# Chunked attention and a gated feed-forward layer: transposes of tiles 14 to 23 by transfers on SP's queue, memory rows on GpSimd's queue, last product in 384 + 128 columns

## Chip, core and metric

The kernel runs on one core of a Trainium2 chip. The metric is the device time of one execution in microseconds; the median of several runs is given. A core has TensorE (matmul; PE in the profile, with its weight loads apart as PEld), VectorE (DVE), ScalarE (ACT), GpSimd (POOL) and SyncE (SP). SP and GpSimd issue transfers, which 16 DMA engines carry out.

## What is computed

Attention in chunks of 32 queries, each over 8 memory keys and a window of 16 + 32 + 8 keys, and then a feed-forward layer over all tokens:

```python
# B, H, S, D = 4, 8, 768, 64; chunk 32, left 16, right 8, n_mem 8
for c in range(S // 32):
    q_c = q[:, :, c_start:c_end]
    k_full = concatenate([mem_k, k[:, :, l_start:r_end]], axis=2)
    v_full = concatenate([mem_v, v[:, :, l_start:r_end]], axis=2)
    scores = scale * matmul(q_c, k_full.T)
    a = exp(scores - max(scores)); a = a / (sum(a) + 1e-09)
    out[:, :, c_start:c_end] = matmul(a, v_full)
x = out.transpose(0, 2, 1, 3).reshape(3072, 512)
result = (maximum(x @ w_gate, 0) * (x @ w_val)) @ w_out      # w_gate, w_val 512x1536, w_out 1536x512
```

## The kernel before

The 3072 tokens are 24 tiles of 128, six to a batch. **Attention of a tile a** has these steps, each one operation of the planner (lines 400 to 428):

- q and k of the tile are loaded by GpSimd's queue, cast to bf16 (`load_qk`, line 185; 18 buffers).
- `t`: four transposes on TensorE into PSUM (`qk_t`, line 206, matmul line 210), one set for k (i = 1) and one for q (i = 0).
- `tc`: a copy from PSUM by ACT or DVE into qT, or into kT with gaps for the memory keys (`qk_copy`, line 212; the copies show as lines 75 and 77).
- `s`: scores (line 236), 32 small products; they need q and k of the tile and k of the next one in the batch.
- maximum, difference, exponential, sum, reciprocal and normalisation on DVE and ACT (lines 241 to 279).
- `p` and `pc`: four transposes of the normalised probabilities (line 285) and the copy from PSUM (`p_copy`, line 287; six buffers).
- `v` and `x`: values (line 298), 16 products against a block-diagonal v, and the copy into xT (`x_copy`, line 301; two buffers, one for each block in work).

The block-diagonal v (`v_bd`, two sets, by batch in turn) is filled by loads on GpSimd's queue (line 167), and its eight memory rows by copies within SBUF on SP's queue, eight for a batch (`mem_rows`, line 138; batch 0 gets its rows from a pattern).

**The feed-forward part** works on blocks of tiles, `BLOCKS = [3, 3, 4, 4, 4, 4, 2]`. For each of twelve hidden columns m of a block there are four products for the gate and four for the value (`first`, line 317, matmul line 323), a relu on ACT (line 329) and a gating product on DVE (line 335). After them come, for each tile of the block, twelve products with w_out (`second`, line 339, matmul line 344, 512 columns wide), a copy on ACT and a store on SP's queue (`store`, line 347; three buffers). The columns of blocks 0 and 1 are worked in turn, in groups of three, as the weights arrive. Four PSUM buffers hold these products, two (`aps`) the transposes, memory keys and values, and one the scores.

**The order** is made by a planner in Python (`schedule`, line 524) while the program is built: each operation has an engine, a cost, what it depends on, a priority and the buffers that it takes and gives. The planner keeps a clock, and an engine that is free takes the ready operation of the best priority; attention (1) comes before feed-forward products (2). On TensorE an attention operation has to have been ready for `MARGIN = 0.4` us after 36 us. The order that results is fixed on each engine: on the chip an engine works its own list and waits where something is late. GpSimd's loads follow a list of their own (lines 481 to 519), with a booked time in the queue for each: 1.05 us for a tile of q or k. `pace` (line 396) holds the transposes of a tile back, in the planner's clock alone, until a column of the block before is at hand:

```python
def pace(a):
    blk = block_of[a]
    return [("f", blk - 1, NDC * (a - starts[blk]) // BLOCKS[blk], 0)] if blk > 1 else []
```

SP's list holds the loads at the start, the memory rows of batches 1 to 3 and the 24 stores.

Of the kernel before, what the change touches and what calls it, by code (L numbers as in the profile page):

```python
# [20 lines left out]
def kernel(  # L21
# [31 lines left out]
    EARLY = TPB  # L53
# [5 lines left out]
    ldpool = ctx.enter_context(tc.tile_pool(name="ldpool", bufs=18))  # L59
    kvpool = ctx.enter_context(tc.tile_pool(name="kvpool", bufs=2))  # L60
# [77 lines left out]
    def mem_rows(b):  # L138
        for par in range(2):
            p = slice(64 * par + CTX, 64 * par + CTX + NMEM)  # L140
            for hp in range(HP):
                src = vmem[p, b, HP * par + hp]
                nc.sync.dma_start(
                    v_bd[b % NSET][p, hp, :, D * par:D * par + D],
                    bass.AP(tensor=src.tensor, offset=src.offset,
                            ap=[src.ap[0], [0, NCH], [1, D]]))
# [59 lines left out]
    def qk_t(a, i):  # L206
        ps = TMP["qk", a, i] = aps.tile([128, HP, 128], BF16, tag="aps", name="qk_ps")
        x = qk_b.pop((a, i))
        for hp in range(HP):
            nc.tensor.transpose(ps[:, hp, :], x[:, 2 * hp:2 * hp + 2, :].rearrange("p h d -> p (h d)"), ident_b)  # L210

# [74 lines left out]

    def p_copy(a, eng):
        PT[a] = smpool.tile([128, HP, 128], F16, name="pT", bufs=6)
        copy(eng, PT[a], TMP.pop(("p", a)))
# [49 lines left out]
    def second(blk, t, m0):  # L339
        st = FFN[blk]  # L340
        if m0 == 0:
            st["o", t] = fps.tile([128, DM], F32, tag="fps", name="out_ps")
        for m in range(m0, m0 + MS):
            nc.tensor.matmul(st["o", t], lhsT=st["gv"][:, m, 128 * t:128 * t + 128],  # L344
                             rhs=w_out_sb[:, m, :], start=(m == 0), stop=(m == NDC - 1))

    def store(blk, t, eng):
        o = opool.tile([128, DM], F32, name="o_sb")
        copy(eng, o, FFN[blk].pop(("o", t)))
        row = 128 * (starts[blk] + t)  # L350
        nc.sync.dma_start(out[row:row + 128, :], o)
# [9 lines left out]
            "qk": 18, "xT": 2, "gv": 2, "gr": 3, "o": 3, "kv": 2}  # L361
# [29 lines left out]
    for b in range(B):  # L391
        op(("new", b), {"DVE": 0.4}, lambda e, b=b: new_batch(b), ["kmc"], take=["kv"],
           prio=(-4.5,) if b == 0 else (1, TPB * b - 2, 0), after=[("t", TPB * b - 2, 0)] if b else [])


    def pace(a):
        blk = block_of[a]
        return [("f", blk - 1, NDC * (a - starts[blk]) // BLOCKS[blk], 0)] if blk > 1 else []

    for a in range(NT):  # L400
        b, t = divmod(a, TPB)
        last = t == TPB - 1
        for i in (1, 0):
            op(("t", a, i), {"PE": 0.24}, lambda e, a=a, i=i: qk_t(a, i), [("qk", a, i), "ib", ("new", b)],
               (1, a - i, 0), ["aps"], ["qk"], pace(max(a - i, 0)))
            op(("tc", a, i), psum(HP * 128), lambda e, a=a, i=i: qk_copy(a, i, engine[e]), [("t", a, i)],
               (1, a - i, 0), (), ["aps"])
        op(("s", a), {"PE": 0.36}, lambda e, a=a: scores(a),
           [("tc", a, 0), ("tc", a, 1)] + ([] if last else [("tc", a + 1, 1)]), (1, a, 1), ["sps"],
           ["kv"] if last else [], [("s", a - 1)] if a else [])  # L410
        op(("max", a), {"DVE": 0.74 + (0.2 if t == 0 or last else 0)}, lambda e, a=a: row_max(a), [("s", a)],
           (1, a, 2), ["mx"])
        op(("sub", a), {"DVE": 0.74}, lambda e, a=a: subtract(a), [("max", a)],
           (1, a, 3), ["dif"], ["sps", "mx"])
        op(("exp", a), {"ACT": 1.15}, lambda e, a=a: exponent(a), [("sub", a)], (1, a, 4), ["p"], ["dif"])
        op(("sum", a), {"DVE": 0.74}, lambda e, a=a: row_sum(a), [("exp", a)], (1, a, 5), ["sm"])
        op(("rec", a), {"DVE": 0.24}, lambda e, a=a: reciprocal(a), [("sum", a)], (1, a, 6), ["rinv"], ["sm"])
        op(("nrm", a), {"DVE": 0.74}, lambda e, a=a: normalise(a), [("rec", a)], (1, a, 7), ["pn"], ["p", "rinv"])
        op(("p", a), {"PE": 0.24}, lambda e, a=a: p_t(a), [("nrm", a)], (1, a, 8), ["aps"], ["pn"])
        op(("pc", a), psum(HP * 128), lambda e, a=a: p_copy(a, engine[e]), [("p", a)], (1, a, 9), ["pT"], ["aps"])  # L420
        blk = block_of[a]
        j = a - starts[blk]
        op(("v", a), {"PE": 0.45}, lambda e, a=a: values(a),
           [("pc", a)] + [("vl", b, 0 if b else t // 3, n) for n in range(2 if b else 2 * HP)]
           + ([("mr", b)] if b else []), (1, a, 10), ["aps"] + (["xT"] if j == 0 else []), ["pT"],
           [("v", a - 1)] if a else [])
        op(("x", a), psum(HP * 128), lambda e, a=a: x_copy(a, engine[e]), [("v", a)], (1, a, 11), (), ["aps"],
           [("x", a - 1)] if a else [])


    seq = [(blk, m) for g in range(WG) for blk in range(2) for m in range(GM * g, GM * g + GM)]
    seq += [(0, None), (1, None)]
    for blk in range(2, len(BLOCKS)):
        seq += [(blk, m) for m in range(NDC)] + [(blk, None)]
    for rank, (blk, m) in enumerate(seq):
# [11 lines left out]
        else:  # L447
            for t in range(n):
                for m0 in range(0, NDC, MS):
                    op(("o", blk, t, m0), {"PE": MS * 0.216}, lambda e, blk=blk, t=t, m0=m0: second(blk, t, m0),  # L450
                       [("g", blk, m) for m in range(m0, m0 + MS)] + [("wo", 0 if m0 + MS <= NDC // 2 else 1)], (2, rank, t, m0),
                       ["fps"] if m0 == 0 else [], ["gv"] if (t, m0) == (n - 1, NDC - MS) else [],
                       [("o", blk, t, m0 - MS)] if m0 else [("o", blk, t - 1, NDC - MS)] if t else [])
                op(("oc", blk, t), {"ACT": psum(512)["ACT"]}, lambda e, blk=blk, t=t: store(blk, t, engine[e]),
                   [("o", blk, t, NDC - MS)], (0.5, rank), ["o"], ["fps", ("o", 2.5)])


    def load_qk_op(a, i):
        load(("qk", a, i), 1024, 1.05, lambda: load_qk(a, i), take=["qk"])

    def load_v_op(b, half, par, c0, c1, n, deps, after):
        for i, part in enumerate(reversed(v_parts(b, par, c0, c1))):
            rows = part[3] - part[2]
            load(("vl", b, half, n) if i == 0 else ("vx", b, n), rows * (part[5] - part[4]),
                 rows * (part[5] - part[4]) * 1.15e-3, lambda part=part: load_v_rows(*part), deps, (), after)
# [7 lines left out]
    def load_w_op(g):  # L473
        for w in range(2):
            for par in range(2):
                load(("w", g, w, par), 256, 1.03, lambda g=g, w=w, par=par: load_gate_val(g, w, par))
# [4 lines left out]
    late = [(a, i) for a in range(TPB, NT) for i in (1, 0)]  # L481
    for a, i in ((0, 1), (1, 1), (0, 0)):
        load_qk_op(a, i)
    load("ident", 0, 0, lambda: make_identity(nc, ident_h))
    for a, i in ((1, 0), (2, 1), (2, 0), (3, 1)):
        load_qk_op(a, i)
    load_v_half(0, (0, 1))
    for a, i in ((3, 0), (4, 1)):
        load_qk_op(a, i)
    load_v_half(0, (2, 3))  # L490
    for a, i in ((4, 0), (5, 1), (5, 0)):
        load_qk_op(a, i)
    load_w_op(0)
    load_v_half(1, range(HP))
    load_w_op(1)
    load_zero(0)
    load_w_op(2)
    load_zero(1)
    for a, i in late[:3]:
        load_qk_op(a, i)  # L500
    load_zero(2)
    load_w_op(3)
    load_zero(3)
    for par in range(2):
        load(("vm", par), 256, 0.3, lambda par=par: mem_values(par))
    for a, i in late[3:6]:
        load_qk_op(a, i)
    for i in range(2):
        load(("wo", i), 768, 4.1, lambda i=i: load_out(i))
    for a, i in late[6:9]:  # L510
        load_qk_op(a, i)
    for b in range(1, B):
        deps = [("z", HP - 1)] if b < NSET else [("v", TPB * (b - NSET + 1) - 1)]
        op(("mr", b), {"SP": 5.8}, lambda e, b=b: mem_rows(b),
           deps + [(("vm", 0), 0.2)] + ([("s", TPB * b - 3)] if b >= NSET else []), (0,))
        for par in range(2):
            load_v_op(b, 0, par, 0, HP * NCH, par, [], deps)
        for a, i in late[9 + 12 * (b - 1):21 + 12 * (b - 1)]:
            load_qk_op(a, i)

    def timed(d):
        return isinstance(d, tuple) and len(d) == 2 and isinstance(d[1], float)

    def schedule():
# [29 lines left out]
        while len(started) < len(ops) + len(loads):  # L554
            t = heapq.heappop(times)
            while times and times[0] <= t + 1e-9:
# [6 lines left out]
            while moved:  # L563
                moved = False
                for e in ("POOL", "PE", "ACT", "DVE", "SP"):
# [18 lines left out]
                    else:  # L584
# [17 lines left out]
                        done[key] = end + (0.25 if e == "PE" else 0.08)  # L602
                        fn = lambda o=o, e=e: o["fn"](e)
# [51 lines left out]
```

## Time and profile before

| | |
|---|---|
| median of 3 runs | 254.91 us (254.59 to 255.48) |
| profiled execution: span from first to last instruction | 253.9 us |
| profiled execution: its own time around the span | not on the page |
| mean granted TensorE clock | 0.990 |
| TensorE busy | 233.7 us (92%) |
| DVE, ACT, POOL busy | 140.6, 112.6, 90.0 us |
| chain of work that ended last | PE 71%, POOL 16%, DMA 9% |
| transfers issued by GpSimd (q0) | 106400 packets, 16.61 MB |
| transfers issued by SP (q1) | 8624 packets, 6.97 MB |

The page divides the span into 40 slices of 6.35 us and gives each engine's busy share in tenths. The chain of work follows the last instruction back to what released it. A group of instructions has its count, busy time, mean length, and the idle time of its engine ahead of it with what ended it. SP's and GpSimd's instructions that issue transfers are listed as they are worked; the packets of the transfers stand apart, by queue.

### The profile page before, as it was taken

To read this page: it belongs to the slowest core of one execution; us is meant where nothing else is said; L and a number is where in the kernel's file an instruction comes from. 1 tells how busy PE (TensorE), PEld (TensorE's weight loads), DVE (VectorE), ACT (ScalarE), POOL (GpSimd) and SP (SyncE) were. 2 spreads that over 40 slices of the span, in tenths; PEclk is the share of its full clock that TensorE was granted. 3 is DMA by queue.
4 is the path that set the end of the run, shared out by engine and by line. 5 is a ranking of instruction groups with operands and counts; after the bars stand their busy time and mean duration, and the time that the engine had idled before them with its cause. 6 is when DMAs were issued, how large, how long until landed. Compare 5 with 4: busy or idle time off the path is not lost.

```text
span 253.9 us, 6022 instructions
## 1 busy us (share of the span) xinstructions
PE 233.7 (92%) x2517; PEld 131.2 (52%) x2517; DVE 140.6 (55%) x259; ACT 112.6 (44%) x245; POOL 90.0 (35%) x102
## 2 busy tenths in 40 slices
PE   1777759999899899999999999999999999999993
PEld 0666435666554544554544555545455545454871
DVE  3977662578563238786157886168873174810430
ACT  3465543455334334554253553355345345432421
POOL 8999699994125565588010000000000000000000
PEclk9999998999999999999999999999999999999998
DMA  9999999999999999999992001210001200002102
GB/s 71 103 117 138 159 144 174 156 147 187 144 143 186 183 174 140 138 147 121 157 216 29 0 3 41 85 41 3 0 3 64 104 0 3 1 26 102 43 3 83
DMA packets 115052, 23.97 MB, mean 94 GB/s; under 512 B 106320, under 2 KB 111952, under 8 KB 115024
## 3 DMA queue, kind: packets, MB, share of 16 engines
q0 software_dynamic: 106400, 16.61, 93.8%
q1 hardware_dynamic: 8624, 6.97, 9.6%
q8 instruction: 20, 0.33, 0.6%
q14 instruction: 8, 0.07, 0.1%
HBM read 33.24 MB, written 6.29 MB: 156 GB/s over the span
## 4 chain that ended last, share of the span: by engine, by line
PE 71%; POOL 16%; DMA 9%; issue 1%; DVE 1%; ACT 0%; POOLq 0%
PE out_ps L344 24%; PE v_ps L323 19%; PE g_ps L323 19%; POOL qk_b L189 6%; DMA qk_b<-in_k_dram 6%; DMA v_bd<-in_v_dram 3%; PE xT_ps L298 3%; PE qk_ps L210 3%; POOL v_bd L167 3%; POOL v_bd L115 2%; POOL w_gate_sb L101 2%; POOL w_val_sb L101 2%; PE s_ps L236 2%; PE pT_ps L285 1%; DVE xT L77 1%
## 5 line engine op out<-in xcount | busy, mean ns | idle before, releaser
L323 PE MATMUL g_ps<-xT,w_gate_sb 128*128 128x512 f16 (+2 forms) x336 | 76.7, 351 | 1.3 <-DMA w_gate_sb<-in_moe_w_gate_dram 1.3
L323 PE MATMUL v_ps<-xT,w_val_sb 128*128 128x512 f16 (+2 forms) x336 | 76.6, 351 | 0.9 <-DMA w_val_sb<-in_moe_w_val_dram 0.8
L335 DVE TENSOR_TENSOR gvT<-v_ps,g_relu 128x512 f16<-128x512 f32 (+2 forms) x84 | 51.6, 614 | 43.9 <-PE v_ps L323 30.5
L329 ACT ACTIVATE g_relu<-g_ps 128x512 f16<-128x512 f32 (+2 forms) x84 | 45.0, 536 | 62.7 <-PE g_ps L323 52.5
L344 PE MATMUL out_ps<-w_out_sb,gvT 128*128 128x512 f16 x288 | 66.1, 379 | 0.0
L323 PEld LDWEIGHTS <-w_gate_sb 128*128 128x128 f16 x336 | 31.9, 98 | 28.8 <-issue 2.1
L323 PEld LDWEIGHTS <-w_val_sb 128*128 128x128 f16 x336 | 31.1, 98 | 23.6 <-DMA w_val_sb<-in_moe_w_val_dram 1.0
L344 PEld LDWEIGHTS <-gvT 128*128 128x128 f16 x288 | 26.9, 98 | 28.9
L167 POOL DMA_DIRECT2D v_bd<-in_v_dram x24 | 27.8, 1179 | 6.1 <-issue 5.4
L189 POOL DMA_DIRECT2D qk_b<-in_k_dram x24 | 23.0, 957 | 18.4 <-issue 6.8
L189 POOL DMA_DIRECT2D qk_b<-in_q_dram x24 | 22.5, 938 | 13.9 <-PE qk_ps L210 7.9
L75 ACT COPY o_sb<-out_ps 128x512 f32<-128x512 f32 x24 | 14.0, 584 | 28.9 <-PE out_ps L344 28.7
L264 ACT ACTIVATE p_exp<-dif 128x256 f16<-128x256 f32 (+2 forms) x72 | 19.6, 338 | 11.4 <-DVE dif L256 11.3
L210 PE MATMUL qk_ps<-ident_b,qk_b 128*128 128x128 bf16 x192 | 18.3, 227 | 5.0 <-DMA qk_b<-in_k_dram 2.6
L249 DVE TENSOR_REDUCE mx<-s_ps 128x8 f32<-128x512 f32 x24 | 16.5, 688 | 5.9 <-PE s_ps L236 5.6
L77 DVE CAST xT<-xT_ps 128x512 f16<-128x512 f32 x10 | 6.9, 692 | 21.7 <-PE xT_ps L298 21.6
L210 PEld LDWEIGHTS <-qk_b 128*128 128x128 bf16 x192 | 13.3, 101 | 10.8 <-DMA qk_b<-in_k_dram 3.7
L268 DVE TENSOR_REDUCE sm<-p_exp 128x8 f32<-128x512 f16 x24 | 16.3, 680 | 3.4 <-ACT p_exp L264 3.4
L75 ACT COPY pT<-pT_ps 128x512 f16<-128x512 f16 x19 | 11.1, 585 | 12.8 <-PE pT_ps L285 12.8
L279 DVE TENSOR_TENSOR p_n<-p_exp,rinv 128x512 f16<-128x512 f16 x24 | 16.5, 687 | 0.4
L256 DVE TENSOR_TENSOR dif<-s_ps,mx 128x512 f32<-128x512 f32 x24 | 16.4, 684 | 0.3
L298 PEld LDWEIGHTS <-v_bd 128*128 128x128 f16 x384 | 12.8, 96 | 5.5 <-issue 2.3
(39 smaller groups left out, 131.8 us busy)
## 6 DMA issues: line engine op xcount, KB each, us to landing
out_dram<-o_sb SPq DMA_DIRECT2D x24, 256.0 KB
v_bd<-in_v_dram POOLq DMA_DIRECT2D x5, 672.0 KB, 14.0
qk_b<-in_k_dram POOLq DMA_DIRECT2D x24, 128.0 KB, 7.0
qk_b<-in_q_dram POOLq DMA_DIRECT2D x24, 128.0 KB, 7.5
w_gate_sb<-in_moe_w_gate_dram POOLq DMA_DIRECT2D x8, 192.0 KB, 4.7
w_val_sb<-in_moe_w_val_dram POOLq DMA_DIRECT2D x8, 192.0 KB, 6.2
w_out_sb<-in_moe_w_out_dram POOLq DMA_DIRECT2D x2, 768.0 KB, 10.0
v_bd<-in_v_dram POOLq DMA_DIRECT2D x15, 84.0 KB, 5.1
```

What stands on the lines that cost most here:

```text
L75: nc.scalar.copy(o, i)
L167: nc.gpsimd.dma_start(dst[64 * par + s0:64 * par + s1, c0:c1, D * par:D * par + D], bass.AP(tensor=v.tensor, offset=v[b, HP * par, 0, 0].o ...
L189: nc.gpsimd.dma_start(qk_b[a, i], bass.AP(tensor=x.tensor, offset=x[b, 0, 128 * t, 0].offset, ap=[[D, 128], [S * D, H], [1, D]]))
L210: nc.tensor.transpose(ps[:, hp, :], x[:, 2 * hp:2 * hp + 2, :].rearrange("p h d -> p (h d)"), ident_b)
L249: nc.vector.reduce_max(SM[a, "mx"], s4, axis=AX.X)
L264: nc.scalar.activation(p[:, :, :, s0:s0 + k1 - k0], dif[:, :, :, k0:k1], ACT.Exp, scale=SCALE)
L279: nc.vector.tensor_tensor(out=P_n[a], in0=SM.pop((a, "p")), in1=rinv_b, op=ALU.mult)
L298: nc.tensor.matmul(ps[:, hp, r], lhsT=v_bd[b % NSET][:, hp, 4 * t + g, :], rhs=x[:, hp, r], start=True, stop=True)
L323: nc.tensor.matmul(ps, lhsT=w[:, f, 128 * m:128 * m + 128], rhs=xTs[blk][:, f, :], start=(f == 0), stop=(f == NFC - 1))
L329: nc.scalar.activation(st["r", m], st.pop((0, m)), ACT.Relu)
L335: nc.vector.tensor_tensor(out=st["gv"][:, m, :], in0=st.pop((1, m)), in1=st.pop(("r", m)), op=ALU.mult)
L344: nc.tensor.matmul(st["o", t], lhsT=st["gv"][:, m, 128 * t:128 * t + 128], rhs=w_out_sb[:, m, :], start=(m == 0), stop=(m == NDC - 1))
```

## The change

- Tiles 14 to 23: the `t` and `p` steps become transposing transfers from SBUF to SBUF, issued by SP (`qk_dma`, `p_dma`), and no longer TensorE transposes. q goes into qT directly and p into its buffer, without a copy. k goes into a new buffer (`k_t`, three of them), from which ACT or DVE copies it into kT. The planner books 1.3 us of SP for each, and counts the data as there 2.0 us (`LANDING`) after that.
- Memory rows of batches 2 and 3 are issued by GpSimd, ahead of the v loads of their batch, in place of SP; those of batch 1 stay on SP, as eight operations and not one.
- `pace` lets the transposes of a tile begin eight columns earlier (`LEAD`), counted through the blocks; from block 2 on, as before.
- The last tile's products with w_out are made in 384 columns and then in 128, each with its own copy and store. The store is an operation of its own on SP for all tiles.
- The planner's booked times for loads are smaller (0.87 us for q or k, 0.94 in place of 1.15 ns for each row piece of v, 0.99 in place of 1.03 us for weights), and SP's transfers are added to the queue's booked time. The loads' list is written as a text; apart from the memory rows its order is the same.

```diff
-    EARLY = TPB
+    LEAD = [8, 8, 8, 8, 8, 8, 8, 8]
+    LAST = ((0, 384), (384, 512))
+    BY_DMA = 14
+    BY_DMA_P = 14
+    LANDING = 2.0
...
+    ktpool = ctx.enter_context(tc.tile_pool(name="ktpool", bufs=3))
...
-    def mem_rows(b):
-        for par in range(2):
+    def mem_rows(b, eng, pieces):
+        for par, hp in pieces:
             p = slice(64 * par + CTX, 64 * par + CTX + NMEM)
...
+            src = vmem[p, b, HP * par + hp]
+            eng.dma_start(
...
+    def qk_dma(a, i):
+        b, t = divmod(a, TPB)
+        x = qk_b.pop((a, i)).rearrange("p h d -> p (h d)")
+        if i == 0:
+            o = qT[b][:, :, 128 * t:128 * t + 128]
+        else:
+            o = TMP["qk", a, i] = ktpool.tile([128, HP, 128], BF16, name="k_t")
+        nc.sync.dma_start_transpose(o, x)
...
+    def p_dma(a):
+        PT[a] = smpool.tile([128, HP, 128], F16, name="pT", bufs=6)
+        nc.sync.dma_start_transpose(PT[a], P_n.pop(a).rearrange("p h a s -> p (h a s)"))
...
-    def second(blk, t, m0):
+    def second(blk, t, m0, cols):
...
-            nc.tensor.matmul(st["o", t], lhsT=st["gv"][:, m, 128 * t:128 * t + 128],
-                             rhs=w_out_sb[:, m, :], start=(m == 0), stop=(m == NDC - 1))
...
+            nc.tensor.matmul(st["o", t, cols], lhsT=st["gv"][:, m, 128 * t:128 * t + 128],
+                             rhs=w_out_sb[:, m, slice(*cols)], start=(m == 0), stop=(m == NDC - 1))
...
-        return [("f", blk - 1, NDC * (a - starts[blk]) // BLOCKS[blk], 0)] if blk > 1 else []
+        if starts[blk] < TPB:
+            return []
+        m = NDC * (blk - 1) + NDC * (a - starts[blk]) // BLOCKS[blk] - LEAD[blk]
+        return [("f", *divmod(max(m, 0), NDC), 0)]
...
+            if a < BY_DMA:
...
+            else:
+                op(("t", a, i), {"SP": 1.3}, lambda e, a=a, i=i: qk_dma(a, i), [("qk", a, i), ("new", b)],
+                   (1, a - i, 0), ["kt"] * i, [("qk", LANDING)])
+                if i:
+                    op(("tc", a, i), {"ACT": 0.62, "DVE": 0.3}, lambda e, a=a, i=i: qk_copy(a, i, engine[e]),
+                       [(("t", a, i), LANDING)], (1, a - i, 0), (), ["kt"])
+                else:
+                    op(("tc", a, i), {"PE": 0.01}, lambda e: None, [(("t", a, i), LANDING)], (1, a - i, 0))
...
+            op(("p", a), {"SP": 1.3}, lambda e, a=a: p_dma(a), [("nrm", a)], (1, a, 8), ["pT"], [("pn", LANDING)])
+            op(("pc", a), {"PE": 0.01}, lambda e: None, [(("p", a), LANDING)], (1, a, 9))
...
+            if blk == len(BLOCKS) - 1:
+                pieces[-1:] = [(n - 1, cols) for cols in LAST]
...
+                if b == 1:
+                    op(("mr", b, par, hp), {"SP": 0.72}, lambda e, b=b, x=(par, hp): mem_rows(b, nc.sync, [x]),
+                       batch_deps(b) + [(("vm", 0), 0.2), (("vm", 1), 0.2)], (0, par, hp))
+                else:
+                    load(("mr", b, par, hp), 192, 0.2, lambda b=b, x=(par, hp): mem_rows(b, nc.gpsimd, [x]),
+                         batch_deps(b) + [("vm", 0), ("vm", 1)])
...
+    MOVE = {"t": 1.25, "p": 1.25, "mr": 0.2, "os": 0.7}
...
+                        if e == "SP" and key[0] in MOVE:
+                            queue_end = max(queue_end, t) + MOVE[key[0]]
```

More of the change, by code (lines that the diff above doesn't have):

```diff
@@ L52 @@
     BLOCKS = [3, 3, 4, 4, 4, 4, 2]
-    EARLY = TPB
+    LEAD = [8, 8, 8, 8, 8, 8, 8, 8]
[3 more added lines that the diff above has]
+    LANDING = 2.0
+    LOADS = """k0 k1 q0 i q1 k2 q2 k3 v00 v01 q3 k4 v02 v03 q4 k5 q5 w0 v10 v11 v12 v13 w1 z0 w2 z1
+               k6 q6 k7 z2 w3 z3 m q7 k8 q8 o0 o1 k9 q9 k10 b1 q10 k11 q11 k12 q12 k13 q13 k14
+               q14 k15 q15 k16 m2 b2 q16 k17 q17 k18 q18 k19 q19 k20 q20 k21 q21 k22 m3 b3 q22 k23 q23"""
     KEY_RUNS = ((0, CH, 0), (KW, 64, CH), (CH, KW, CTX))
@@ L136, in mem_values @@
         )
-    def mem_rows(b):
-        for par in range(2):
+    def mem_rows(b, eng, pieces):
+        for par, hp in pieces:
             p = slice(64 * par + CTX, 64 * par + CTX + NMEM)
[L141 to L146, printed above, removed]
+            src = vmem[p, b, HP * par + hp]
+            eng.dma_start(
+                v_bd[b % NSET][p, hp, :, D * par:D * par + D],
+                bass.AP(tensor=src.tensor, offset=src.offset,
+                        ap=[src.ap[0], [0, NCH], [1, D]]))
     def pattern_load():
@@ L337, with out_copy, store @@
     MS = 3
-    def second(blk, t, m0):
+    def second(blk, t, m0, cols):
         st = FFN[blk]
         if m0 == 0:
-            st["o", t] = fps.tile([128, DM], F32, tag="fps", name="out_ps")
+            st["o", t, cols] = fps.tile([128, cols[1] - cols[0]], F32, tag="fps", name="out_ps")
         for m in range(m0, m0 + MS):
-            nc.tensor.matmul(st["o", t], lhsT=st["gv"][:, m, 128 * t:128 * t + 128],
-                             rhs=w_out_sb[:, m, :], start=(m == 0), stop=(m == NDC - 1))
-    def store(blk, t, eng):
-        o = opool.tile([128, DM], F32, name="o_sb")
-        copy(eng, o, FFN[blk].pop(("o", t)))
+            nc.tensor.matmul(st["o", t, cols], lhsT=st["gv"][:, m, 128 * t:128 * t + 128],
+                             rhs=w_out_sb[:, m, slice(*cols)], start=(m == 0), stop=(m == NDC - 1))
+    def out_copy(blk, t, eng, cols):
+        o = opool.tile([128, cols[1] - cols[0]], F32, name="o_sb")
+        copy(eng, o, FFN[blk].pop(("o", t, cols)))
+        FFN[blk]["sb", t, cols] = o
+    def store(blk, t, cols):
         row = 128 * (starts[blk] + t)
-        nc.sync.dma_start(out[row:row + 128, :], o)
+        nc.sync.dma_start(out[row:row + 128, slice(*cols)], FFN[blk].pop(("sb", t, cols)))
     starts = [sum(BLOCKS[:i]) for i in range(len(BLOCKS))]
@@ L360 @@
     room = {"aps": 2, "sps": 1, "fps": 4, "mx": 2, "dif": 2, "p": 2, "sm": 2, "rinv": 2, "pn": 2, "pT": 6,
-            "qk": 18, "xT": 2, "gv": 2, "gr": 3, "o": 3, "kv": 2}
+            "qk": 18, "xT": 2, "gv": 2, "gr": 3, "o": 3, "kv": 2, "kt": 3}
     def op(key, eng, fn, deps=(), prio=(0,), take=(), give=(), after=()):
@@ L392 @@
         op(("new", b), {"DVE": 0.4}, lambda e, b=b: new_batch(b), ["kmc"], take=["kv"],
-           prio=(-4.5,) if b == 0 else (1, TPB * b - 2, 0), after=[("t", TPB * b - 2, 0)] if b else [])
+           prio=(-4.5,) if b == 0 else (1, TPB * b - 2, 0), after=[("tc", TPB * b - 2, 0)] if b else [])
     def pace(a):
         blk = block_of[a]
-        return [("f", blk - 1, NDC * (a - starts[blk]) // BLOCKS[blk], 0)] if blk > 1 else []
+        if starts[blk] < TPB:
+            return []
+        m = NDC * (blk - 1) + NDC * (a - starts[blk]) // BLOCKS[blk] - LEAD[blk]
+        return [("f", *divmod(max(m, 0), NDC), 0)]
     for a in range(NT):
@@ L403 @@
         for i in (1, 0):
[L404 to L407, printed above, removed]
+            if a < BY_DMA:
+                op(("t", a, i), {"PE": 0.24}, lambda e, a=a, i=i: qk_t(a, i), [("qk", a, i), "ib", ("new", b)],
+                   (1, a - i, 0), ["aps"], ["qk"], pace(max(a - i, 0)))
+                op(("tc", a, i), psum(HP * 128), lambda e, a=a, i=i: qk_copy(a, i, engine[e]), [("t", a, i)],
+                   (1, a - i, 0), (), ["aps"])
+            else:
[6 more added lines that the diff above has]
+                    op(("tc", a, i), {"PE": 0.01}, lambda e: None, [(("t", a, i), LANDING)], (1, a - i, 0))
         op(("s", a), {"PE": 0.36}, lambda e, a=a: scores(a),
@@ L418 @@
         op(("nrm", a), {"DVE": 0.74}, lambda e, a=a: normalise(a), [("rec", a)], (1, a, 7), ["pn"], ["p", "rinv"])
-        op(("p", a), {"PE": 0.24}, lambda e, a=a: p_t(a), [("nrm", a)], (1, a, 8), ["aps"], ["pn"])
-        op(("pc", a), psum(HP * 128), lambda e, a=a: p_copy(a, engine[e]), [("p", a)], (1, a, 9), ["pT"], ["aps"])
+        if a < BY_DMA_P:
+            op(("p", a), {"PE": 0.24}, lambda e, a=a: p_t(a), [("nrm", a)], (1, a, 8), ["aps"], ["pn"])
+            op(("pc", a), psum(HP * 128), lambda e, a=a: p_copy(a, engine[e]), [("p", a)], (1, a, 9), ["pT"], ["aps"])
+        else:
+            op(("p", a), {"SP": 1.3}, lambda e, a=a: p_dma(a), [("nrm", a)], (1, a, 8), ["pT"], [("pn", LANDING)])
+            op(("pc", a), {"PE": 0.01}, lambda e: None, [(("p", a), LANDING)], (1, a, 9))
         blk = block_of[a]
@@ L424 @@
            [("pc", a)] + [("vl", b, 0 if b else t // 3, n) for n in range(2 if b else 2 * HP)]
-           + ([("mr", b)] if b else []), (1, a, 10), ["aps"] + (["xT"] if j == 0 else []), ["pT"],
+           + ([(("mr", b, par, hp), 2.0 if b == 1 else 0.0) for par in range(2) for hp in range(HP)] if b else []), (1, a, 10), ["aps"] + (["xT"] if j == 0 else []), ["pT"],
            [("v", a - 1)] if a else [])
@@ L428 @@
            [("x", a - 1)] if a else [])
-    seq = [(blk, m) for g in range(WG) for blk in range(2) for m in range(GM * g, GM * g + GM)]
-    seq += [(0, None), (1, None)]
-    for blk in range(2, len(BLOCKS)):
+    n_early = sum(x < TPB for x in starts)
+    seq = [(blk, m) for g in range(WG) for blk in range(n_early) for m in range(GM * g, GM * g + GM)]
+    seq += [(blk, None) for blk in range(n_early)]
+    for blk in range(n_early, len(BLOCKS)):
         seq += [(blk, m) for m in range(NDC)] + [(blk, None)]
@@ L447 @@
         else:
-            for t in range(n):
-                for m0 in range(0, NDC, MS):
[L450 to L455, printed above, removed]
+            pieces = [(t, (0, DM)) for t in range(n)]
+            if blk == len(BLOCKS) - 1:
+                pieces[-1:] = [(n - 1, cols) for cols in LAST]
+            before = None
+            for t, cols in pieces:
+                for m0 in range(0, NDC, MS):
+                    op(("o", blk, t, m0, cols), {"PE": MS * (0.0025 + (cols[1] - cols[0]) / 2400)},
+                       lambda e, blk=blk, t=t, m0=m0, cols=cols: second(blk, t, m0, cols),
+                       [("g", blk, m) for m in range(m0, m0 + MS)] + [("wo", 0 if m0 + MS <= NDC // 2 else 1)], (2, rank, t, cols, m0),
+                       ["fps"] if m0 == 0 else [], ["gv"] if (t, cols, m0) == (*pieces[-1], NDC - MS) else [],
+                       [before] if before else [])
+                    before = ("o", blk, t, m0, cols)
+                op(("oc", blk, t, cols), {"ACT": psum(cols[1] - cols[0])["ACT"]},
+                   lambda e, blk=blk, t=t, cols=cols: out_copy(blk, t, engine[e], cols),
+                   [before], (0.5, rank), ["o"], ["fps"])
+                op(("os", blk, t, cols), {"SP": 0.4}, lambda e, blk=blk, t=t, cols=cols: store(blk, t, cols),
+                   [("oc", blk, t, cols)], (0.5, rank), (), [("o", 2.5)])
     def load_qk_op(a, i):
-        load(("qk", a, i), 1024, 1.05, lambda: load_qk(a, i), take=["qk"])
+        load(("qk", a, i), 1024, 0.87, lambda: load_qk(a, i), take=["qk"])
     def load_v_op(b, half, par, c0, c1, n, deps, after):
@@ L464, in load_v_op @@
             load(("vl", b, half, n) if i == 0 else ("vx", b, n), rows * (part[5] - part[4]),
-                 rows * (part[5] - part[4]) * 1.15e-3, lambda part=part: load_v_rows(*part), deps, (), after)
+                 rows * (part[5] - part[4]) * 0.94e-3, lambda part=part: load_v_rows(*part), deps, (), after)
     def load_v_half(half, hps):
@@ L475, in load_w_op @@
             for par in range(2):
-                load(("w", g, w, par), 256, 1.03, lambda g=g, w=w, par=par: load_gate_val(g, w, par))
+                load(("w", g, w, par), 256, 0.99, lambda g=g, w=w, par=par: load_gate_val(g, w, par))
     def load_zero(hp):
         load(("z", hp), 0, 1.5, lambda: zero(nc.gpsimd, v_bd[1], hp))
[L481 to L515, printed above, removed]
-        for par in range(2):
-            load_v_op(b, 0, par, 0, HP * NCH, par, [], deps)
-        for a, i in late[9 + 12 * (b - 1):21 + 12 * (b - 1)]:
-            load_qk_op(a, i)
+    def batch_deps(b):
+        return [("z", HP - 1)] if b < NSET else [("v", TPB * (b - NSET + 1) - 1)]
@@ new lines, in load_batch, with load_memory @@
+    def load_batch(b):
+        for par in range(2):
+            load_v_op(b, 0, par, 0, HP * NCH, par, [], batch_deps(b))
+    def load_memory(b):
+        for par in range(2):
+            for hp in range(HP):
+                if b == 1:
+                    op(("mr", b, par, hp), {"SP": 0.72}, lambda e, b=b, x=(par, hp): mem_rows(b, nc.sync, [x]),
+                       batch_deps(b) + [(("vm", 0), 0.2), (("vm", 1), 0.2)], (0, par, hp))
+                else:
+                    load(("mr", b, par, hp), 192, 0.2, lambda b=b, x=(par, hp): mem_rows(b, nc.gpsimd, [x]),
+                         batch_deps(b) + [("vm", 0), ("vm", 1)])
@@ new lines, in load_by @@
+    def load_by(name):
+        what, n = name[0], int(name[1:] or 0)
+        if what in "qk":
+            load_qk_op(n, "qk".index(what))
+        elif what == "i":
+            load("ident", 0, 0, lambda: make_identity(nc, ident_h))
+        elif what == "v":
+            load_v_half(n // 10, [n % 10])
+        elif what == "w":
+            load_w_op(n)
+        elif what == "z":
+            load_zero(n)
+        elif what == "m" and n:
+            load_memory(n)
+        elif what == "m":
+            for par in range(2):
+                load(("vm", par), 256, 0.3, lambda par=par: mem_values(par))
+            load_memory(1)
+        elif what == "o":
+            load(("wo", n), 768, 4.1, lambda n=n: load_out(n))
+        elif what == "b":
+            load_batch(n)
@@ L521, in timed @@
+    for name in LOADS.split():
+        load_by(name)
     def timed(d):
         return isinstance(d, tuple) and len(d) == 2 and isinstance(d[1], float)
+    MOVE = {"t": 1.25, "p": 1.25, "mr": 0.2, "os": 0.7}
     def schedule():
@@ L555, in schedule @@
             t = heapq.heappop(times)
+            assert t < 400.0
             while times and times[0] <= t + 1e-9:
```

## The prediction, made before the changed kernel ran

> **What bounds it now.** I read the page's engine totals and its 40 slices first, then the chain of work that ended last in order of time, then the rows by shape, and last the queues of SP and GpSimd.
>
> ```profile
> PE 233.7 (92%) x2517; PEld 131.2 (52%) x2517; DVE 140.6 (55%) x259; ACT 112.6 (44%) x245; POOL 90.0 (35%) x102
> PE   1777759999899899999999999999999999999993
> POOL 8999699994125565588010000000000000000000
> PEclk9999998999999999999999999999999999999998
> DMA  9999999999999999999992001210001200002102
> ```
>
> A slice is 6.35 us. TensorE has holes in the first six slices (to 38 us), where loads arrive one after another, and is full from there to the end at a full clock. The transfers that GpSimd issues fill the DMA engines to about slice 21 (133 us); after that they are almost idle. The chain says what the full TensorE does:
>
> ```profile
> 127.18 0.86 PE g_ps L323 x4
> 128.04 0.45 PE qk_ps L210 x8
> 128.49 0.86 PE v_ps L323 x4
> 129.35 0.86 PE g_ps L323 x4
> 130.21 0.24 PE s_ps L236 x32
> 130.45 0.97 PE v_ps L323 x4
> ...
> 138.26 0.22 PE pT_ps L285 x4
> ```
>
> Each piece starts where the last one ends, and four products of 512 columns take 0.86 us. Attention pieces stand between those of the feed-forward part, and each of their microseconds is one of the end. From 36 us on the matmul starts show four holes, of 0.6, 0.8, 0.3 and 0.7 us (at 36.5, 66.7, 85.4 and 86.3), 2.4 in all; after 90 us there is none. So TensorE work taken out after 90 us shortens the kernel one for one, as long as nothing makes TensorE wait in its place.
>
> **Transposes off TensorE.** Tiles 14 to 23 are ten tiles with a set for q, one for k and one for p, of four transposes each: 120.
>
> ```profile
> L210 PE MATMUL qk_ps<-ident_b,qk_b 128*128 128x128 bf16 x192 | 18.3, 227 | 5.0 <-DMA qk_b<-in_k_dram 2.6 <-DMA qk_b<-in_q_dram 2.3
> L285 PE MATMUL pT_ps<-ident_h,p_n 128*128 128x128 f16 x96 | 9.3, 219 | 1.7 <-DVE p_n L279 1.3 <-ACT xT L75 0.3
> ```
>
> The 227 and 219 ns are pipelined durations; what counts is the distance of starts, 0.45 us for eight in the chain, 56 ns each. 120 x 0.056 = **6.7 us**.
> [...]
>
> With them go 20 copies from PSUM (q and p; 0.58 us on ACT or 0.43 on DVE). The ten of k stay, now from SBUF; nearest row: 0.42 us on DVE. DVE (55%) and ACT (44%) do not bound: 0. The two PSUM buffers that transposes, keys and values share are freed too: 0.
>
> **What the transfers cost.** No row has a transposing transfer of SP. For the issue, a store is 0.33 us and a broadcast row of 192 pieces 0.69 to 3.70:
>
> ```profile
> L351 SPq DMA_DIRECT2D out_dram<-o_sb x24: 332/332/378, 74.3 to 250.7; - x24
> L143 SPq DMA_DIRECT2D v_bd<-vmem x24: 685/751/3696, 51.7 to 134.5; - x24
> 119.03 9.17 SPq L351 DMA_DIRECT2D out_dram<-o_sb  x4
> 155.66 9.29 SPq L351 DMA_DIRECT2D out_dram<-o_sb  x4
> ```
>
> The planner books 1.3 us, between these ends; I take that. Thirty take 39 us of SP in some 125 us, with 14 stores at 0.33 beside them: SP is not full.
> For the time from issue to landing, the packets of the stores are the nearest row. The store issued at 155.66, with the loads over, moved its packets from 156.49 to 157.31 (1.65 us in all). The one issued at 119.03, beside the loads, began at 122.57 and ended at 125.5 (6.5 us); those of 80 to 91 us, also beside loads, took 2.4 to 4.8. So 1.65 to 6.5 us. Outside the loads I take 1.3 of issue and about 1.2 behind it, 2.5.
>
> **The new wait.** The order is fixed on each engine. The values of a tile (line 298) stand in TensorE's order where the planner thinks p is there: 1.3 + 0.08 + 2.0 landing + 0.4 margin = 3.8 us after SP begins. All feed-forward products stand behind them, so a later landing is idle time on TensorE one for one. Behind a waiting p transfer on SP stand the next transposes and stores; a held store keeps one of three output buffers. q and k are safer: SP does not obey the planner's pacing, only data, so it starts them when the load is there and the place in SP's order is free. A late k would hold the copy on DVE and the gates behind it.
> At 2.5 us the ten waits after the loads cost nothing (1.3 us of cover each). Beside the loads there are about four tiles, 14 to 17, as the pace is now eight hidden columns earlier (1.73 us each, 14 us) and the loads run to 133 us or later. Tile 14 is covered, because its values need a buffer of xT that block 2 holds until its last first product (near 114 us). For three, 0 to 6.5 - 3.8 = 2.7 us each, 0 to 8 us. The stores nearest to a transfer of half their size are those of 2.4 to 4.8 us, mean 3.4 and under the cover, with a tail above. I take **1.3 us**.
> [...]
>
> **Memory rows.** Batches 2 and 3 leave SP (16 issues, the last eight at 128.29 to 135.29) and enter GpSimd's queue ahead of the values of v. Nearest rows there: 0.56 us (a small v_bd load) to 0.85 (L132). Eight at 0.7 are 5.6 us, and loads behind them come up to that much later. The v loads of batch 2, issued at 90.09 and 94.04 with 14.0 us to landing, come by 108 and would by 114; block 3 is first used at 127.2. Cover 13 us: 0. Without it, 5.6 us once per batch. From SP go eight transfers issued between 62 and 71 us, where the loads are late: between 0 and -0.8 (the hole at 66.7).
>
> **Pace, load costs.** The order of the loads stays. Attention earlier in a full TensorE moves work and removes none; it can close holes (to -1.8 beyond the 0.8 above) or make others where attention now meets loads that have just landed (66 to 100 us). q, k and v loads are booked 18% cheaper; 1024 pieces of the trace pass in 0.90 us at its best rate (5700 in 5 us), which fits the new 0.87 better than 1.05. Bounds -2.4 to +3; I take 0.
>
> **The end.** The last copy takes 0.59 us for 512 columns, then a store, with packets of 2048 bytes for 0.82 us.
>
> ```profile
> 250.05 0.59 ACT L75 COPY o_sb<-out_ps 128x512 f32<-128x512 f32 x1 [2.00 <-PE out_ps L344]
> ```
>
> For 128 columns the copy lies between 0.243 (64, exp) and 0.384 (256, relu): 0.29, saving 0.3. The packets, 128 of 512 bytes, lie between 0.36 (256 bytes, start of the kernel) and 0.82: 0.45, saving 0.4. The same columns in twelve more products add 12 x 3 ns. The 384 columns are copied while the last 128 are computed, 0.67 us. Net **-0.7** (0 to -0.8).
>
> **Sum.** -6.7 - 0.7 + 1.3 = -6.1. The profiled span of 253.9 becomes 247.8; the page has no time of that execution around its span, and the median of the runs, 254.9, is 1.0 above it. Forecast **248.8**, own range 246 to 251.5.
>
> **Rivals.**
> 1. Holes close as well and no transfer is late: 254.9 - 6.7 - 0.7 - 2.4 = 245.1. For it: the earlier pace. Against: the holes are set by loads whose order stays. 0.08.
> 2. The gain is mostly swapped for waits: the three tiles pay most of the 8 us, or the early part loses 3: 251.5 to 254, middle 253. For it: the 6.5 us store. 0.12.
> 3. It does not do what it says: p lands about 4.4 us after its issue begins in all ten tiles, TensorE idles 10 x 0.7 in place of 6.7, about 255. 0.05.
> 4. Slower: p's landing ahead of the values. Above 3.8 us each microsecond counts once per tile, and ten tiles lose the gain at 3.8 + 7.4/10 = 4.5 us. At the 6.5 of the loaded store, four tiles with tile 14 uncovered give 247.5 + 4 x 2.7 = 258; ten give 274. For it: no row shows a transposing transfer. Against: DMA engines idle after 133 us. 0.18, of it 0.07 beyond 258, which also takes a costlier issue on SP.
> 5. Transposes are worth their 219 ns: 120 x 0.219 = 26 us, 228. Against: the chain. 0.01.
>
> My forecast has 0.56. Faster by over 0.3% (below 254.1; about what a measurement can tell from no change) is 0.56 + 0.08 + 0.12 + 0.01 = 0.77, within it 0.05, slower 0.18. The range of 8 in 10 goes from 245 to 257, into rival 4 for the uncosted landing.
>
> **What the trace will show.** qk_ps x112 and pT_ps x56 on TensorE. Chain almost all PE after 90 us, without qk_ps or pT_ps behind tile 13; a wait of xT_ps on a DMA is rival 2, 3 or 4, by its sum. SP's transposes near 1.3 us; twice that is rival 4. Last copy near 0.3 us. v_bd of batch 2 landed before block 3's first product. What would make this wrong: a transfer that lands later than 3.8 us outside the loads, or TensorE waiting on loads between 66 and 100 us.

## The result and the profile after

The changed kernel takes 267.05 us in the median of four runs (264.34 to 268.19), the kernel before 255.09 beside it: ratio 1.046, 95% interval [1.040, 1.052]. The forecast was 248.8, with a range of 245 to 257. Some executions fall into a slower state; the ratios here and below leave them out and the medians do not, so that the two can differ (two of the four without the lead). The profiled execution took 267.68 us, 265.9 of them span: 12.0 us more than the span before.

The same lines of the page as before, from the changed kernel:

```profile
PE 233.7 (88%) x2407; PEld 128.7 (48%) x2407; DVE 132.8 (50%) x247; ACT 108.6 (41%) x238; POOL 100.1 (38%) x118
PE   1867949999999949999746969999999999999995
POOL 8999699963457682584840000000000000000000
PEclk9998989999999997999995989999999999999999
DMA  9999999999999999999999992233100120002202
```

A slice is 6.65 us here. TensorE is no longer full: it has holes in slices 15 and 20 to 24 (93 to 160 us) and none from there to the attention's end. The granted clock drops to 0.5 in slice 22. The DMA engines stay full until about 160 us and not 133. TensorE's busy time is the 233.7 us of before although 120 transposes are gone, because products start 0.43 us apart and not 0.22 in some stretches of half clock. The chain of work, in order of time, shows what stands in the hole:

```profile
132.24 11.60 DMA pT<-p_n
143.84 0.04 issue
143.88 0.58 PE xT_ps L318 x16
144.47 1.71 PE g_ps L343 x4
```

One transposing transfer of p lies on the chain for 11.6 us, and the four products behind it take 1.71 us, where the same piece took 0.86 before. A copy of k out of its new buffer (timeline; in brackets the engine's idle time ahead and what ended it) and the scores behind it:

```profile
140.80 0.62 ACT L83 COPY kT<-k_t 128x512 bf16<-128x512 bf16 x1 [7.87 <-DMA k_t<-qk_b]
141.47 0.39 PE L252 MATMUL s_ps<-kT,qT 64*32 64x64 bf16 x26 [5.57 <-ACT kT L83]
```

ACT stood still for 7.9 us until k had landed, and TensorE 5.6 us for ACT. In all, TensorE waited longer for k than for p (its waits: total, times, longest):

```profile
PE s_ps L252 <- ACT kT L83: 7.0, 3, 5.6
PE xT_ps L318 <- DMA pT<-p_n: 3.1, 3, 1.7
```

Another 3.6 us of scores waited for DVE, which a copy of k had held for 4.2 us. SP's list gives three of the issues of p:

```profile
122.40 1.19 SPq L305 DMA_TRANSPOSE pT<-p_n  x1
132.24 4.64 SPq L305 DMA_TRANSPOSE pT<-p_n  x1
171.39 1.19 SPq L305 DMA_TRANSPOSE pT<-p_n  x1
```

An undisturbed issue takes 1.19 us. By the landing records of the trace, the transfer issued at 122.40 landed after 8.65 us, that of 132.24 after 11.6, that of 171.39 after 2.39. Of the thirty, 22 were issued beside the loads and landed after 4.1 to 11.6 us, median 8.2; one issued at 158.1, as the last loads came in, after 3.6; the seven behind it after 2.4.

### The profile page after: what moved, and what is told of

Its sections match the earlier page's. It is cut to its first block, busy times and chain, and to the rows that moved or that the text cites. A ratio compares the mean times of both kernels' runs of the same rounds, so it can differ in the third digit from the quotient of the medians.

```text
span 265.9 us, 5867 instructions
## 1 busy us (share of the span) xinstructions
PE 233.7 (88%) x2407; PEld 128.7 (48%) x2407; DVE 132.8 (50%) x247; ACT 108.6 (41%) x238; POOL 100.1 (38%) x118
## 4 chain that ended last, share of the span: by engine, by line
PE 46%; DMA 35%; POOL 12%; issue 6%; ACT 0%; POOLq 0%; DVE 0%
PE v_ps L343 15%; PE g_ps L343 15%; PE out_ps L364 14%; DMA v_bd<-in_v_dram 10%; DMA pT<-p_n 8%; POOL qk_b L196 6%; DMA qk_b<-in_k_dram 6%; POOL v_bd L174 4%; DMA qk_b<-in_q_dram 4%; DMA k_t<-qk_b 3%; DMA w_val_sb<-in_moe_w_val_dram 2%; DMA v_bd<-vmem 2%; PE xT_ps L318 1%; POOL w_gate_sb L109 1%; POOL w_val_sb L109 1%
## 5 line engine op out<-in xcount | busy, mean ns | idle before, releaser
L343 PE MATMUL v_ps<-xT,w_val_sb 128*128 128x512 f16 (+2 forms) x336 | 79.6, 362 | 1.1 <-DMA w_val_sb<-in_moe_w_val_dram 1.1
L343 PE MATMUL g_ps<-xT,w_gate_sb 128*128 128x512 f16 (+2 forms) x336 | 78.6, 358 | 1.8 <-DMA w_gate_sb<-in_moe_w_gate_dram 1.5
L364 PE MATMUL out_ps<-w_out_sb,gvT 128*128 128x512 f16 (+2 forms) x300 | 66.3, 371 | 0.0
L343 PEld LDWEIGHTS <-w_gate_sb 128*128 128x128 f16 x336 | 32.8, 100 | 31.6 <-issue 5.5
L343 PEld LDWEIGHTS <-w_val_sb 128*128 128x128 f16 x336 | 32.4, 100 | 29.4 <-issue 4.3
L83 ACT COPY o_sb<-out_ps 128x512 f32<-128x512 f32 (+2 forms) x25 | 14.2, 567 | 29.1 <-PE out_ps L364 28.0
L252 PE MATMUL s_ps<-kT,qT 64*32 64x64 bf16 (+2 forms) x768 | 8.5, 198 | 11.5 <-ACT kT L83 7.0
L318 PE MATMUL xT_ps<-pT,v_bd 128*128 128x32 f16 x384 | 13.4, 178 | 5.4 <-DMA pT<-p_n 3.1
L83 ACT CAST xT<-xT_ps 128x512 f16<-128x512 f32 x19 | 11.1, 585 | 16.9 <-PE xT_ps L318 16.6
L217 PE MATMUL qk_ps<-ident_b,qk_b 128*128 128x128 bf16 x112 | 11.9, 238 | 4.1 <-DMA qk_b<-in_q_dram 3.1
```

The source lines that it names most:

```text
L83: nc.scalar.copy(o, i)
L318: nc.tensor.matmul(ps[:, hp, r], lhsT=v_bd[b % NSET][:, hp, 4 * t + g, :], rhs=x[:, hp, r], start=True, stop=True)
L343: nc.tensor.matmul(ps, lhsT=w[:, f, 128 * m:128 * m + 128], rhs=xTs[blk][:, f, :], start=(f == 0), stop=(f == NFC - 1))
L364: nc.tensor.matmul(st["o", t, cols], lhsT=st["gv"][:, m, 128 * t:128 * t + 128], rhs=w_out_sb[:, m, slice(*cols)], start=(m == 0), stop=(m ...
```

## The experiments

Theory A: the transposing transfers meet GpSimd's loads on the DMA engines and land far later than the 2.0 us behind the issue that the planner books; since every engine works a fixed order, engines wait and TensorE idles. Rival B: the memory rows on GpSimd's queue hold up the loads. Rival C: the earlier pace makes TensorE meet fresh loads. Ratios are against the kernel before on the same chip, with 95% intervals; the times beside them are medians.

| kernel | us | ratio |
|---|---|---|
| changed kernel | 267.05 | 1.046 [1.040, 1.052] |
| all transposes on TensorE | 254.14 | 0.996 [0.993, 1.000] |
| rows on SP | 267.64 | 1.042 [1.033, 1.050] |
| no lead | 263.86 | 1.022 [1.016, 1.028] |
| booked landing 8 | 251.40 | 0.987 [0.981, 0.993] |
| only p by transfer | 258.54 | 1.014 [1.009, 1.019] |
| only q and k by transfer | 266.73 | 1.047 [1.042, 1.052] |
| booked landing 12 | 247.89 | 0.973 [0.967, 0.979] |
| booked landing 8, rows on SP | 255.10 | 0.996 [0.992, 1.001] |
| from tile 21 | 255.02 | 0.998 [0.995, 1.001] |
| from tile 10, landing 12 | 268.98 | 1.054 [1.049, 1.059] |
| booked landing 16 | 254.72 | 0.999 [0.996, 1.003] |
| booked landing 12, no lead | 247.62 | 0.969 [0.964, 0.973] |

**All transposes on TensorE.**

```diff
-    BY_DMA = 14
-    BY_DMA_P = 14
+    BY_DMA = 24
+    BY_DMA_P = 24
```


> Of the changed kernel, only the 30 transposing transfers are undone: tiles 14 to 23 are transposed by TensorE again. Theory A (the transposes on SP's queue, issued while the loads run, land 4 to 11.6 us after their issue where the order allows 3.8, and TensorE idles in its fixed order): the four holes of 2 to 6 us between 95 and 157 us and the half-clock stretches behind them go, 6.7 us of transposes come back, 253 to 256 us. Theory B (the memory rows in GpSimd's queue hold up the loads, and TensorE waits for loads): the holes stay in large part, 258 us or more.


254.14 us, and no hole on TensorE after 40 us. The whole loss comes with the transfers, and B falls. All other parts of the change together are worth 0.4%, between 0 and 0.7%.

**Memory rows of all batches on SP.**

```diff
-                if b == 1:
+                if b >= 1:
...
-                       batch_deps(b) + [(("vm", 0), 0.2), (("vm", 1), 0.2)], (0, par, hp))
+                       batch_deps(b) + [(("vm", 0), 0.2), (("vm", 1), 0.2)]
+                       + ([("s", TPB * b - 3)] if b >= NSET else []), (0, par, hp))
```


> Of the changed kernel, only the memory rows of batches 2 and 3 go back to SP's queue. Theory A: the transposes still meet the loads, 262 us or more, with landing of the transposes still over 4 us up to the end of the loads. Theory B: the 5.7 us in which nothing but memory rows lands in GpSimd's queue (93.4 to 99.1 and 126.3 to 131.9 us) go, the loads end 10 us earlier or more (161 before), and the time falls to 256 us or below.


267.64 us. The last load landed at 152.1 us and not at 161.2, nearly the 10 us of B, and the time did not follow. B falls a second time.

**No lead.**

```diff
-    LEAD = [8, 8, 8, 8, 8, 8, 8, 8]
+    LEAD = [0, 0, 0, 0, 0, 0, 0, 0]
```


> Of the changed kernel, only the pace is set back to no lead (LEAD 0). The first transposes come some 14 us later and fewer of them beside the loads. Theory A: fewer late landings, so a good part of the 17 us of holes goes, 252 to 260 us. Theory C (the lead makes TensorE meet loads of q and k that have just come, the transfers being blameless): the holes go wholly, about 248 us. Theory B: no change, 265.


By the ratio 260.6 us, from two runs: about half of the loss stays, with holes of 2.6, 2.0 and 4.7 us. C falls as the sole cause; A's range ended just below, at 260.

**Booked landing of 8 us.**

```diff
-    LANDING = 2.0
+    LANDING = 8.0
```


> Of the changed kernel, only the planner's booked landing of a transposing transfer is 8.0 us and not 2.0: the transfers are the same, but scores and values stand later in TensorE's order. Theory A with the fixed order as the cause of the loss: most of the holes go, 248 to 254 us. If the loss is in the loads that the transposes slow down (v of batch 3 landed 26 us after its issue), the holes stay: 260 us or more.


251.40 us, 15.7 less than the changed kernel, by the order alone. The transfers landed as late as ever (21 of them after 5.4 to 10.0 us, median 8.1), and the loads ended at 158 us. So the loss was not the slow transfers themselves but where the fixed order put their readers.

**Only p, and only q and k** (booked 2.0 us, as in the changed kernel).

```diff
-    BY_DMA = 14
+    BY_DMA = 24
```


> Of the changed kernel, q and k of all tiles are transposed by TensorE again; the ten transfers of p stay, booked at 2.0 us. The prediction held p to be the exposed one and k to be safe, since SP runs ahead. If so, this keeps the loss: 260 us or more. If the late k transposes (holes of 4.0 and 5.8 us ahead of the scores at 95.6 and 135.7 us in the changed kernel) are the larger part, or if it takes all thirty transfers to crowd the loads, it comes to 250 to 256 us, with single holes ahead of the values.

```diff
-    BY_DMA_P = 14
+    BY_DMA_P = 24
```


> Of the changed kernel, p of all tiles is transposed by TensorE again; the twenty transfers of q and k stay, booked at 2.0 us. If p is the exposed one, 250 to 253 us (4.5 us of transposes gone, few holes). If k is exposed as well, holes ahead of the scores and 256 us or more.


Only p: 258.54 us, between the two expectations. With twenty transfers fewer the loads end at 145 us, and three of the ten transfers meet them (4.8, 3.0 and 10.3 us to landing). One hole is left after 40 us, ahead of values:

```profile
PE xT_ps L318 <- DMA pT<-p_n: 4.2, 1, 4.2
```

Only q and k: 266.73 us, the whole loss. So p is exposed, but q and k are more so. The timeline around its largest hole:

```profile
144.38 0.62 ACT L83 COPY kT<-k_t 128x512 bf16<-128x512 bf16 x1 [9.97 <-DMA k_t<-qk_b]
144.91 0.58 ACT L83 COPY o_sb<-out_ps 128x512 f32<-128x512 f32 x1
145.38 0.60 ACT L349 ACTIVATE g_relu<-g_ps 128x512 f16<-128x512 f32 x1
145.53 1.87 PE L343 MATMUL v_ps<-xT,w_val_sb 128*128 128x512 f16 x4 [7.93 <-ACT o_sb L83]
```

No score waits here. ACT's next entry is a copy of k that has not landed; the output copy and the relu behind it, both with their data ready, wait 10 us, no product's PSUM buffer comes free, and TensorE stops for 7.9 us.

**Booked landing of 12 us.**

```diff
-    LANDING = 2.0
+    LANDING = 12.0
```


> As the run with 8.0 us of booked landing, which kept holes of 1.0 and 2.5 us at 146 and 148 us from transfers that landed after 8 to 10 us, but with 12.0. If a booked landing above the real one is all that is missing: no hole after 90 us, 246 to 249 us. If the later places in the order bring waits of another kind (buffers, the end of the attention), 251 or more.


247.89 us, 2.7% faster than before, with no hole over 0.7 us after 40 us:

```profile
PE 228.4 (93%) x2407; PEld 128.3 (52%) x2407; DVE 135.1 (55%) x250; ACT 107.0 (44%) x235; POOL 100.0 (41%) x118
PE   1786978999999999999999999999999999999994
PEclk9999797999999999999999999999999999999999
DMA  8999999999999999999999999983103200012102
```

The DMA engines are as crowded as in the changed kernel (21 transfers landed after 6.3 to 11.1 us, median 8.2), and all copies of k together waited 0.7 us for them. TensorE's busy time is 5.3 us under that of before.

**Booked landing of 8 us with the rows on SP** (the two diffs together).


> As the run with 8.0 us of booked landing, with the memory rows of batches 2 and 3 back on SP's queue. If the rows in GpSimd's queue cost nothing (they alone changed nothing in the changed kernel), 251 us as without; if they prolong the loads and so the crowded time, 248 to 250 us with the last load landed before 150 us and not at 158.


255.10 us: neither. The loads ended at 154 us and not 158, and the holes moved to other places (86 to 155 us, none over 1.7). By the ratios the rows on SP cost about 2 us here and nothing in the changed kernel; why stays open.

**Transfers from tile 21** (`BY_DMA = BY_DMA_P = 21`, booked 2.0).


> Of the changed kernel, the transposing transfers begin with tile 21 and not 14 (nine transfers, 2.0 us of TensorE saved), still booked at 2.0 us. The stores of block 3 stand ahead of them in SP's order, so they are issued when the loads have ended. If the loads are what makes the transfers late, each lands 2.4 us after its issue, there is no hole after 90 us, and the time is that of the run with all transposes on TensorE less 2: 252 us. If the booked 2.0 is too short by itself, single holes ahead of the values of tiles 21 to 23 stay: 254 or more.


255.02 us. The expectation was wrong on when they are issued: q and k stand ahead of block 2's last stores in SP's order, and three of these six transfers went out as soon as their loads had landed, at 119.9 to 122.8 us, beside the other loads, with 4.0 to 4.9 us to landing.

```profile
119.93 1.31 SPq L226 DMA_TRANSPOSE k_t<-qk_b  x1
124.54 1.25 DVE L85 COPY kT<-k_t 128x512 bf16<-128x512 bf16 x1 [5.01 <-DMA k_t<-qk_b]
128.46 0.40 PE L301 MATMUL pT_ps<-ident_h,p_n 128*128 128x128 f16 x4 [2.75 <-DVE p_n L295]
```

This k, of tile 21, is first needed by the scores of tile 20, at 157 us. It held DVE for 5.0 us, the softmax of an earlier tile stood behind it, and TensorE waited 2.75 us for that. The three p, issued after 169 us, landed after 3.6, 2.4 and 2.4 us and held nothing up. So the transfers are late beside the loads, and without them they stay within the booked place.

**Transfers from tile 10, booked 12 us** (`BY_DMA = BY_DMA_P = 10`).


> As the run with 12.0 us of booked landing, which had no hole over 0.7 us, but the transfers begin with tile 10: 48 more transposes leave TensorE, 2.7 us. If TensorE's work is still all that counts, 245 us. If twelve more transfers beside the loads push landings over 12 us or the loads behind their first use, holes come back: 248 us or more.


268.98 us, the second expectation. The last load lands at 171.5, and scores wait again:

```profile
PE s_ps L252 <- ACT kT L83: 5.6, 1, 5.6
PE s_ps L252 <- DMA qT<-qk_b: 4.8, 1, 4.8
```

Late landings are not what these two waits show. The q of 4.8 us was loaded only at 124.5 us; its transfer went out at once and landed 7.1 us later, within the 12 booked (one of the 42 took 12.2). In the other, ACT stood 9.6 us at an output copy until a store had landed, with the copy of k behind it. More transfers also delay loads and stores, which the booked landing does not cover.

**Booked landing of 16 us.**


> As the run with 12.0 us of booked landing, with 16.0. The landings beside the loads were 6 to 11 us there, so no more than the 1.3 us of holes can be gained: 246.5 to 248.5 us. If the later places run into the end of the attention or into the three buffers of k, 249 or more.


254.72 us: the second expectation. The values now come too late for the next block, whose first product waits for the copy into xT:

```profile
PE g_ps L343 <- ACT xT L83: 3.9, 2, 3.1
```

**Booked landing of 12 us without the lead** (the two diffs together).


> As the run with 12.0 us of booked landing, without the lead of eight columns in the pace. The chain of one tile from the start of its transposes to its values is then 24 us longer than with none of the landing booked, and a block's first product needs its four tiles. If the lead is what pays for the long landing, TensorE runs out of products at block ends: 250 us or more. If it is of no use, 248.


247.62 us, no different from 247.89 with the lead. The lead does not pay for the long landing.

## Why the prediction was wrong, step by step

- **Transposes off TensorE: right.** 112 and 56 transposes remain as forecast; where next to nothing waits (landing 12) the kernel is 7.1 us faster than before, against 6.7 + 0.7 forecast. Against the run with all transposes on TensorE it is 5.8 us by the ratios, against 6.7.
- **The end: right.** From the start of the last copy to the end of the span it is 3.1 us after 3.8; the copy took 0.27:

```profile
262.75 0.27 ACT L83 COPY o_sb<-out_ps 128x128 f32<-128x128 f32 x1 [0.19 <-PE out_ps L364]
```

- **Transfers alone: right.** 1.19 us of issue (1.3 taken) and 2.4 to landing (2.5 taken).
- **"The stores nearest to a transfer of half their size are those of 2.4 to 4.8 us, mean 3.4 and under the cover": wrong, and the first step that failed.** These times fit the end of the burst of packets that follows each issue. In three of the four stores only half of the landing's sixteen steps had come with that burst, by 2.8 to 3.7 us; the other half came with the next, from 5.4 us on. A reader waits for all sixteen: in the changed kernel the steps of the k issued at 130.19 us came from 138.7 to 140.78, and ACT's copy of it began at 140.80. The landing records of the kernel before had it: these four stores landed after 5.2 to 5.6 us, those of 119 to 128 after 5.9 to 7.5, and 2.0 alone. All the loaded ones are over the 3.8 us of cover. Measured for the transfers: median 8.2. So the term of 1.3 us for the new wait came out at about 17 (below).
- **"Beside the loads there are about four tiles, 14 to 17": wrong.** 22 of 30 transfers met them, and tile 14, held to be covered, waited 1.7 us for its p. SP runs ahead of the pace, which the prediction took for a safeguard and which is what brings the transfers into the crowd; and they slow the loads in turn (last landing at 161 us, 144 with all transposes on TensorE; the last three loads landed 25 to 27 us after their issue, and 14 there).
- **"q and k are safer": wrong, and the largest part.** Alone they give the whole loss. "A late k would hold the copy on DVE and the gates behind it" was written down and not priced; what is queued behind the waiting copy on ACT and DVE is the products' own outlet. p alone has a smaller part: 1.014 against 0.996 with all transposes on TensorE.
- **Holes cost more than their length: not in the sum.** The starts of TensorE's products after 36 us show 20.1 us over the normal distance, and 2.6 before. Some 5 us of it are 24 products at 0.43 us and not 0.22, behind holes.
- **Memory rows at 0: right** for the changed kernel. **Pace and load costs at 0:** the 49th of the products for the hidden columns starts at 44.0 us, 43.1 before. In runs whose edits come later in the kernel it starts between 42.8 (landing 12) and 45.3 (transposes on TensorE), so that this 0.9 is not shown to be a cost. The pace brought part of the crowding (1.046 against 1.022 without).

The sum afterwards: -6.7 - 0.7 + 17.5 (20.1 - 2.6, in place of 1.3) + 0.9 = 11.0 of the 12.0 us. The two last terms overlap between 36 and 44 us, so that the sum is good to a microsecond at best, and the last one is not accounted for. The slower rival named the place (a landing behind the fixed order), but for p alone. Its two sizes, 258 for four tiles and 274 for ten, lie on either side of the measured time; a time beyond 258 had a chance of 0.07.

## What to carry to other kernels

In an order that is fixed beforehand, a transfer costs next to nothing as long as its reader stands behind its real landing, and a wait if it does not: 2.0 us booked gave 267, 12.0 gave 248, with the same transfers. Booking more than that costs too: 16.0 gave 255. Take the time from the moment the reader is released, not from the first packets that follow the issue, and from the stage in which the transfer will really be issued, which a queue that runs ahead can move into the crowd (2.4 us to landing with the loads over, a median of 8.2 beside them). For each new wait, price what stands behind it on its own engine: a copy that nobody needs yet can close the outlet of the engine that bounds (7.9 us of TensorE with only q and k by transfer).

## What the runs showed of the hardware

The profile by stages (the column after POOL is TensorE's granted clock) shows what follows a hole:

```profile
95.00:100.00 5.00, 1.39 (x38) 0.56 (x37) 4.13 (x7) 0.57 (x2) 5.00 (x4) 0.92 1.73 160
100.00:105.00 5.00, 5.00 (x21) 2.15 (x22) 2.96 (x7) 1.49 (x6) 1.58 (x2) 0.74 2.33 137
135.00:147.00 12.00, 6.23 (x63) 2.51 (x62) 3.85 (x8) 2.89 (x7) 0.67 (x1) 0.72 2.07 131
```

These are stages of the changed kernel. After TensorE's hole of 4.0 us at 95.6 the clock was at half from 99.2 to 102.6 us, after that of 5.8 us at 135.7 from 140.1 to 147.0. The length of a hole alone does not tell: one of 2.1 us at 129.0 was not followed by such a stretch, while two of 1.2 and 1.6 us at 153 and 155 were, from 157.2 to 160.6. What decides it was not shown.
